# Sending a quarter of one w_down tile's rows over five of the sixteen DMA engines in a decode layer

## The chip, the core and the metric

The kernel runs on one core of a Trainium2 chip. The metric is device time in microseconds (us) of one execution, and lower is better. PE is the matrix engine, DVE the vector engine, ACT the scalar engine, POOL is GpSimd, and SP is the engine whose queue issues nearly all transfers. The core's transfers are carried by 16 DMA engines, which each take the packets handed to them in order.

## What is computed

One decode step for one token, with an attention branch and a gated feed-forward branch in parallel. All data are float32.

```python
xn = layernorm(x)                                  # x: 1 x 1 x 1024
q = (xn @ wq)                                      # 32 heads of 128
k, v = last 4096 rows of the caches                # 4 key/value heads, each used by 8 query heads
a = softmax(q k^T * 128**-0.5) v @ wo              # wo: 4096 x 1024
h = gelu(xn @ w_gate) * (xn @ w_up)                # 1024 -> 3584
out = x + a + h @ w_down                           # w_down: 3584 x 1024
```

Every weight and every cache row is used once, so about 94 MB have to come from HBM, and each loaded byte is used in one product with a vector.

## The kernel before

**Loads.** All weights and caches pass through one ring of five slots in SBUF (`ring`, 128 partitions x 40960 floats). The table `PLAN` gives for each load its place in the ring and the load whose place it takes: when the work on that older load has been written out, `used` calls `load`, which issues the transfer on SP's queue. SP waits there until the engines have read the old contents. In order these are wq in two halves, keys and values in two halves interleaved with w_gate, then w_up, wo (`oa`, `ob`, then `o1`) and at the end w_down (`d0`, `d1`, `d2`). A load of 128 partitions keeps all 16 DMA engines busy.

**w_down.** Its 3584 rows are 28 tiles of 128 rows, one row of 1024 floats (4 KB) in each partition. `d0` holds tiles 0 to 15, `d1` 16 to 23 in two pieces, `d2` 24 to 27. `PIECES` cuts `d2` into tiles 24 and 25 together (8 KB in a partition), tile 26, and tile 27, which comes in three column pieces of 2 KB, 1 KB and 1 KB in a partition.

**Products with a vector.** A tile times its scalar per partition goes one of two ways. On DVE, `add_scaled` multiplies a tile by a column and adds it to the running sum `out_part` in SBUF (one instruction for a tile of 1024 columns). On PE, `accumulate_halves` or `accumulate` multiply the tile by a column of a mostly zero matrix (`hz` for h, `oz` for the heads) and sum in PSUM. `WO_KEPT` lists the even tiles of each half of wo that go to DVE beside the odd ones; `KEPT` does so for `d0`. `downs` then adds the PE sums, takes the last tiles as they land, and `store` sends the result out in four small transfers.

**Order.** The program is written out by hand, and every engine executes its own instructions in that order. `Flow` finds the reads and writes that depend on each other and puts in semaphore waits. Where one instruction needs several semaphores, further wait instructions stand ahead of it.

**Buffers.** `Pool.tile` gives tiles of the same tag the same place, one after the other. `part` holds DVE's sums over wq, w_gate and w_up; its last reader before the end is the PE work of `projected("u")`.

Of the kernel before, what the change touches and what calls it, by code (L numbers as in the profile page):

```python
# [5 lines left out]
F32 = mybir.dt.float32  # L6
# [5 lines left out]
P = 128  # L12
D = 1024
# [5 lines left out]
NR = 4  # L19
# [9 lines left out]
WIDTHS = (NB, P // 4 * SHORT)  # L29
PIECES = ((0, 16), (0, 4, 8), (0, 2, 3, 4))  # L30
KEPT = (1, 3, 5, 7, 9, 11)
WO_KEPT = ((2, 4, 6, 10, 12, 14), (2, 4, 6, 10, 12, 14))
PAIRED = 18
# [10 lines left out]
ROW = (31, 32, 95, 96)  # L44
SIZES = {"tp": 2 * NB, "acc": 2 * NB, "s": 2 * NB, "o": 2 * NB, "part": 8 * NB, "rows": 2 * NB, "pT": 2 * NB, "p": 2 * NB}

# [193 lines left out]
class Pool:  # L240
# [33 lines left out]
    (("oa", 0), 4 * SLOT, ("g", 1)), (("ob", 0), 0, ("u", 0)), (("o", 1), SLOT, ("ua", 1)),  # L274
    (("d", 0), 3 * SLOT, ("oa", 0)), (("d", 1), 0, ("ob", 0)),
    (("d", 2), SLOT, ("o", 1)),
# [3 lines left out]
def decode_layer(nc, x, k_cache, v_cache, wq, wo, w_gate, w_up, w_down, out):  # L280
# [35 lines left out]
    def load(key, at):  # L316
        kind, i = key
        src = source(*key)
        if kind in "kv":

            loaded[key] = dst = ring[:, at:at + SLOT]
            if kind == "v":
                nc.sync.dma_start(dst, src)
            else:
                for odd in range(2):
                    nc.sync.dma_start(dst[odd:P:2], src[:, odd])
            return
        rows, n = src.shape[1:]
        loaded[key] = ring[:, at:at + rows * n]
        dst = loaded[key].rearrange("p (t n) -> p t n", n=n)  # L330
        pieces = PIECES[i] if kind == "d" else (0, rows)
        for t, end in zip(pieces, pieces[1:]):
            ends = (0, n // 2, 3 * n // 4, n) if key == ("d", 2) and end == rows else (0, n)
            for cols in (slice(*cut) for cut in zip(ends, ends[1:])):
                nc.sync.dma_start(dst[:, t:end, cols], src[:, t:end, cols])

    def used(key):
# [8 lines left out]
    for j in range(NJ):  # L346
        nc.scalar.dma_start(x_rows[j:j + 1, :], x_in[j:j + 1, :])
    sizes = (CO, NR * NJ * 32, 8 * P, (TD + 1) * 32, (HQ + 1) * 32, 2 * 32)
    zeros = consts.tile([P, sum(sizes)], F32, name="zeros")
    nc.vector.memset(zeros, 0.0)  # L350
    ends = [sum(sizes[:k]) for k in range(len(sizes) + 1)]
    x_out, xz, qz, hz, oz, units = (zeros[:, a:b] for a, b in zip(ends, ends[1:]))
    xz = xz.rearrange("p (r j m) -> p r j m", j=NJ, m=32)
# [16 lines left out]


    nc.vector.memset(units[:, 0, 31:32], 1.0)
    unit = units[:, 0, :]

    same = consts.tile([P, 4, 32], F32, name="same")
    nc.vector.tensor_add(same[:, 0, :], ident[:, 0:32], ident[:, 64:96])
    nc.vector.tensor_add(same[:, 1, :], ident[:, 32:64], ident[:, 96:128])
    quad = consts.tile([P, 4], F32, name="quad")
    nc.vector.reduce_sum(quad, ident.rearrange("p (a k) -> p a k", a=4), axis=AX.X)
# [103 lines left out]
    def queries():  # L483
        q_t = work.tile([P, 2 * 4 * 4, 32], F32, name="q_t", tag="rows")
        nc.vector.transpose(q_t.rearrange("p t r -> p (t r)"), acc["q"].rearrange("p b n -> p (b n)"))
# [63 lines left out]
    def exponentials(g, s):  # L549
        p = work.tile([P, 2, NB], F32, name="p", bufs=2)  # L550
        for odd in range(2):
            nc.scalar.activation(
                p.rearrange("p b (n odd) -> p odd (b n)", odd=2)[:, odd], s[:, odd], AF.Exp,
                bias=bias[:, g, odd:odd + 1], scale=SCALE, accum_out=l[:, g, odd:odd + 1],
            )
        probs[g] = p
# [46 lines left out]
    def heads():  # L603
        o_sb = work.tile([P, 2, DH], F32, name="o_sb", tag="p", bufs=2)
        for g in range(2):
# [6 lines left out]
        yield  # L612
        own = work.tile([P, 2, 8, WIDE], F32, name="own", tag="rows")
        nc.vector.tensor_mul(
# [10 lines left out]
    g_sb = work.tile([P, 2, NB], F32, name="g_sb", tag="pT")  # L625
    h_sb = work.tile([P, 2, NB], F32, name="h_sb")

    def gelu():
        t_sb = work.tile([P, 2, NB], F32, name="t_sb", tag="rows")
        cut = [(g_sb[:, b, :n], t_sb[:, b, :n], h_sb[:, b, :n]) for b, n in enumerate(WIDTHS)]  # L630
# [15 lines left out]
    def hidden():  # L646
# [4 lines left out]
        for b, count in enumerate((LONG, SHORT)):  # L651
            rows = h_sb[:, b, :32 * count].rearrange("p (k t) -> p t k", t=count)
            nc.vector.transpose(hz[:, t:t + count, :], rows)
            t += count

    out_p = psum.tile([P, CO], F32, name="out_p", tag="o")
    half_p = psum.tile([P, NB], F32, name="half_p", tag="s")
    halves = []
    out_part = work.tile([P, D], F32, name="out_part", tag="p")
    y = work.tile([P, CO], F32, name="y")  # L660
# [49 lines left out]
    def downs():  # L710

        tiles = [loaded["d", i][:, n * D:(n + 1) * D] for i in range(3) for n in range(DOWN[i])]
        for t in KEPT:
            add_scaled(out_part, tiles[t], hz[:, t, 31:32], False)
# [41 lines left out]
    for key, _, _ in PLAN:  # L756
        kind, i = key
        if kind == "q":
            project("q", i, loaded.pop(key), range(NR), 8 * NB)
# [56 lines left out]
        elif kind[0] == "o":  # L816
            outputs(key)
            if kind == "oa":
                gated()
            elif kind == "ob":  # L820
                hidden()
        elif i == 2:
            downs()
# [29 lines left out]
```

## Time and profile before

| | before |
|---|---|
| median of 3 runs | 226.77 us (226.47 to 226.92) |
| profiled execution, its own time | 226.74 us |
| its span, first to last instruction | 225.2 us |
| PE busy | 101.3 us (45%) |
| DVE busy | 168.2 us (75%) |
| ACT busy | 16.8 us (7%) |
| POOL busy | 0.7 us |
| DMA, data queue's packets, share of 16 engines | 97.6% |
| read from HBM | 94.38 MB, 419 GB/s over the span |

The span lies inside the execution; 1.5 us of the profiled execution's time lie outside it. Busy time is the union of an engine's instructions. The DMA share is the mean over 16 engines, so that a share of 0.25 late in the span means that four of them have packets and twelve have none. A packet counts in the stretch in which it starts, which is why a short stretch can show a share a little over 1. All rows carry L237, the line of the helper through which every instruction is issued, so they are told apart by tile names: `p<-ring,zeros,p` is `add_scaled` into `out_part` (here in the place of tag `p`), `s<-ring,zeros` is `accumulate_halves`, `o<-ring,zeros` is `accumulate`. The trace shows a float32 matmul as two MATMUL and two LDWEIGHTS.

### The profile page before, as it was taken

Reading aid. Unit: us, or ns where it says so; the run is one execution under the profiler, and the core shown is the slowest. Engines: PE = TensorE matmul, PEld = TensorE weight load, DVE = VectorE, ACT = ScalarE, POOL = GpSimd, SP = SyncE. Lnnn points to the kernel's source line nnn. Section 1 sums busy time; section 2 is a strip of 40 time slices with the busy share of each in tenths; the row PEclk is TensorE's granted clock in tenths of the full one; section 3 lists DMA queues with packets and bytes.
Section 4 is the critical chain, followed back from the end, with each engine's and each line's share of the span. In section 5 each row is a group of like instructions: output and inputs, shape, how many; then the busy total and the mean of one; then the engine's idle time right before and its main releaser. Section 6 shows DMA issues by size and latency. Waiting matters only on the chain.

```text
span 225.2 us, 1136 instructions
## 1 busy us (share of the span) xinstructions
PE 101.3 (45%) x430; PEld 37.5 (17%) x430; DVE 168.2 (75%) x148; ACT 16.8 (7%) x45; POOL 0.7 (0%) x6
## 2 busy tenths in 40 slices
PE   0120000544899999799979460010016003000986
PEld 0010000111343434243424110000001000000232
DVE  7130998598905476945439969999999998998982
ACT  0120000000102040102040140000000000000000
POOL 1000000000000000000000000000000000000000
PEclk9999999999589999999999855555556655555599
DMA  9889889799997999999989989999999989988993
GB/s 373 373 384 548 373 373 559 343 402 466 442 489 326 422 460 450 390 496 407 479 357 471 469 346 458 423 450 402 448 460 396 524 384 396 524 384 375 425 409 121
DMA packets 3236, 94.44 MB, mean 419 GB/s; under 512 B 398, under 2 KB 670, under 8 KB 928
## 3 DMA queue, kind: packets, MB, share of 16 engines
q1 hardware_dynamic: 3208, 94.38, 97.6%
q8 instruction: 3, 0.05, 0.1%
q10 hardware_dynamic: 24, 0.01, 0.0%
q14 instruction: 1, 0.01, 0.0%
HBM read 94.38 MB, written 0.00 MB: 419 GB/s over the span
## 4 chain that ended last, share of the span: by engine, by line
DMA 61%; DVE 25%; PE 11%; SPq 1%; issue 0%; ACT 0%; DVEq 0%
DVE part L237 19%; DMA ring<-in_A_wq 18%; DMA ring<-in_A_k_cache 17%; DMA ring<-in_B_w_down 13%; DMA ring<-in_A_wo 13%; PE o L237 4%; PE tp L237 3%; PE s L237 3%; DVE ring L237 2%; DVE p L237 2%; PE acc L237 1%; DVE rows L237 1%; DVE pT L237 1%; SPq L237 1%; ACT pT L237 0%
## 5 line engine op out<-in xcount | busy, mean ns | idle before, releaser
L237 DVE SCALAR_TENSOR_TENSOR part<-ring,zeros,part 128x3584 f32<-128x3584 f32 (+1 forms) x16 | 65.8, 4112 | 3.7 <-DMA ring<-in_A_wq 3.4
L237 DVE SCALAR_TENSOR_TENSOR p<-ring,zeros,p 128x1024 f32<-128x1024 f32 x34 | 43.7, 1285 | 3.2 <-DMA ring<-in_B_w_down 1.3
L237 PE MATMUL s<-ring,zeros 128*32 128x512 f32 (+1 forms) x96 | 29.1, 826 | 36.6 <-DMA ring<-in_B_w_down 17.5
L237 PE MATMUL o<-ring,pT 128*128 128x512 f32 x64 | 29.1, 599 | 1.3 <-DVE pT L237 1.3
L237 PE MATMUL acc<-ring,zeros 128*32 128x512 f32 (+2 forms) x88 | 11.4, 646 | 28.6 <-DMA ring<-in_A_wq 28.6
L237 DVE STREAM_TRANSPOSE ring<-ring 128x4096 f32<-128x4096 f32 (+1 forms) x5 | 17.7, 3571 | 2.8 <-DMA ring<-in_A_k_cache 2.8
L237 PEld LDWEIGHTS s<-ring,zeros 128*32 128x32 f32 (+1 forms) x96 | 9.7, 175 | 55.5 <-DVE p L237 19.2
L237 PE MATMUL acc<-part,zeros 128*32 128x512 f32 (+1 forms) x48 | 8.4, 835 | 21.7 <-DVE part L237 21.7
L237 PE MATMUL tp<-ring,zeros 128*128 128x512 f32 (+1 forms) x40 | 15.3, 536 | 0.0
L237 PEld LDWEIGHTS o<-ring,pT 128*128 128x128 f32 x64 | 11.7, 190 | 15.9 <-issue 13.8
L237 DVE TENSOR_SCALAR part<-ring,zeros 128x3584 f32<-128x3584 f32 (+1 forms) x3 | 6.5, 2172 | 8.6 <-DMA ring<-in_A_wq 7.6
L237 DVE STREAM_TRANSPOSE pT<-p 128x1024 f32<-128x1024 f32 x4 | 5.0, 1246 | 7.0 <-PE o L237 3.9
L237 PE MATMUL tp<-p,pick 128*128 128x256 f32 x2 | 1.2, 715 | 18.3 <-DVE p L237 18.3
L237 PEld LDWEIGHTS acc<-ring,zeros 128*32 128x32 f32 x88 | 3.1, 127 | 36.2 <-issue 35.8
L237 DVE TENSOR_REDUCE m<-s 128x2 f32<-128x1024 f32 x2 | 2.4, 1224 | 8.4 <-PE s L237 8.4
L237 PEld LDWEIGHTS tp<-ring,zeros 128*128 128x128 f32 (+1 forms) x40 | 5.9, 173 | 6.3 <-issue 5.7
L237 PEld LDWEIGHTS acc<-part,zeros 128*32 128x32 f32 x48 | 1.6, 142 | 27.2 <-DVE part L237 24.0
L237 ACT ACTIVATE o_raw<-o 32x128 f32<-32x128 f32 x16 | 4.3, 269 | 20.5 <-PE o L237 20.4
L237 PE MATMUL tp<-ident,pT 2*128 2x2 f32 x4 | 0.6, 252 | 10.3 <-DMA pT<-in_A_x 10.3
L237 PE MATMUL o<-ring,zeros 128*32 128x256 f32 x64 | 4.3, 384 | 1.6 <-DMA ring<-in_B_w_down 1.6
L237 DVE TENSOR_REDUCE m<-tp 128x2 f32<-128x1024 f32 x2 | 2.4, 1224 | 3.1 <-PE tp L237 3.1
L237 ACT ACTIVATE p<-s,bias 128x512 f32<-128x512 f32 x4 | 2.8, 715 | 24.3 <-DVE bias L237 24.3
(87 smaller groups left out, 49.1 us busy)
## 6 DMA issues: line engine op xcount, KB each, us to landing
ring<-in_B_w_gate SPq DMA_DIRECT2D x2, 7168.0 KB, 28.8
ring<-in_A_k_cache SPq DMA_DIRECT2D x4, 2048.0 KB, 41.4
ring<-in_A_v_cache SPq DMA_DIRECT2D x2, 4096.0 KB, 28.0
ring<-in_A_wo SPq DMA_DIRECT2D x2, 4096.0 KB, 27.5
ring<-in_B_w_up SPq DMA_DIRECT2D x1, 7168.0 KB, 27.8
ring<-in_B_w_up SPq DMA_DIRECT2D x2, 3584.0 KB, 21.4
ring<-in_B_w_down SPq DMA_DIRECT2D x2, 2048.0 KB, 31.7
ring<-in_B_w_down SPq DMA_DIRECT2D x1, 1024.0 KB, 29.6
```

The lines of the kernel that those rows point to most:

```text
L237: return lambda *a, **k: self.flow.issue(self.engine, lambda: call(*a, **k))
```

## The change

Tile 24 (the first tile of `d2`) is loaded in another way. Of its 128 rows, those in partitions 3, 7, 11, ... (32 of them) no longer come with the tile. They come earlier, between `o1` and `d0` on SP's queue, into the buffer `part`: six transfers of 5 rows and one of 2 rows, each row 4 KB. A transfer of 5 rows is meant for DMA engines 0 to 4, one row each, and the one of 2 rows for engines 0 and 1. The other 96 rows of the tile come in two transfers, one of 64 partitions (every second) and one of 32 (1, 5, 9, ...); the 32 missing partitions are set to zero by POOL ahead of them. So the first piece of `d2` becomes tile 24 alone, and tiles 25 and 26 come together.

The moved rows get their own product: `where`, a 0/1 matrix that POOL builds at the start, brings the h values of these rows to the partitions in which they now lie (one small matmul, `hidden_moved`, and one copy by ACT into `moved_h`), and DVE adds them to `out_part` with one more `add_scaled` on 64 partitions, ahead of those for `d0`. POOL sets `part` to zero before the rows come in.

`WO_KEPT` for the second half of wo loses tiles 4, 10 and 12, which go to PE. The kernel no longer asks for a DMA scratch of 4096 bytes for GpSimd and takes the default. To make room, buffers share places: `hz` lies over `qz`, the two buffers of tag `p` become `p0` and `p1` and also hold what `rows`, `h_sb` and `out_part` held, and `own` lies in `y`.

```diff
-PIECES = ((0, 16), (0, 4, 8), (0, 2, 3, 4))
+PIECES = ((0, 16), (0, 4, 8), (0, 1, 3, 4))
-WO_KEPT = ((2, 4, 6, 10, 12, 14), (2, 4, 6, 10, 12, 14))
+WO_KEPT = ((2, 4, 6, 10, 12, 14), (2, 6, 14))
...
+OWN, EACH, STEP = 5, 7, 4
+AWAY = 1
...
-    (("d", 0), 3 * SLOT, ("oa", 0)), (("d", 1), 0, ("ob", 0)),
+    (("m", 0), None, ("ub", 1)), (("d", 0), 3 * SLOT, ("oa", 0)), (("d", 1), 0, ("ob", 0)),
...
+        if kind == "m":
+            load_moved()
+            return
...
+        if key == ("d", 2):
+            nc.gpsimd.memset(loaded[key][:, :AWAY * n], 0.0)
+            for t, end in zip(pieces, pieces[1:2]):
+                part_of = src[:, t:end].rearrange("p t n -> p (t n)")
+                for some in (slice(0, P, 2), slice(1, P, 4)):
+                    nc.sync.dma_start(loaded[key][some, t * n:end * n], part_of[some])
+            pieces = pieces[1:]
...
+    def load_moved():
+        moved.append(work.tile([P, AWAY, D], F32, name="moved", tag="part"))
+        there = moved[0].rearrange("p t n -> p (t n)")
+        nc.gpsimd.memset(there[:64], 0.0)
+        rest = w_down[P * LONG:, :].rearrange("(p r) n -> p (r n)", r=SHORT)[STEP - 1::STEP]
+        cols = slice(DOWN[1] * D, (DOWN[1] + AWAY) * D)
+        for j in range(EACH):
+            rows = rest[OWN * j:min(OWN * j + OWN, P // STEP), cols]
+            to = 32 * (j // 4) + j % 4
+            nc.sync.dma_start(there[to:to + 4 * rows.shape[0]:4], rows)
...
-    sizes = (CO, NR * NJ * 32, 8 * P, (TD + 1) * 32, (HQ + 1) * 32, 2 * 32)
+    sizes = (CO, NR * NJ * 32, 8 * P, 32, (HQ + 1) * 32, 2 * 32)
...
+    where = consts.tile([P, 2, 8, 4], F32, name="where")
+    nc.gpsimd.memset(where, 0.0)
+    taken = ident[:, STEP - 1::STEP]
+    for j in range(EACH):
+        rows = taken[:, OWN * j:min(OWN * j + OWN, P // STEP)]
+        nc.gpsimd.tensor_copy(where[:, j // 4, :rows.shape[1], j % 4], rows)
...
+    def hidden_moved():
+        h_p = small("h_p")
+        t = DOWN[0] + DOWN[1]
+        r = slice(0, 64)
+        nc.tensor.matmul(
+            h_p[r, :AWAY], where.rearrange("p h e j -> p (h e j)"), hz[:, t:t + AWAY, 31],
+            start=True, stop=True,
+        )
+        nc.scalar.activation(moved_h[r], h_p[r, :AWAY], AF.Copy)
...
+        n = 64
+        for s in range(AWAY):
+            add_scaled(out_part[:n], moved[0][:n, s], moved_h[:n, s:s + 1], False)
         for t in KEPT:
             add_scaled(out_part, tiles[t], hz[:, t, 31:32], False)
...
-        nc = bacc.Bacc(
-            "TRN2", target_bir_lowering=False, num_devices=1, dynamic_dma_scratch_size=4096
-        )
+        nc = bacc.Bacc("TRN2", target_bir_lowering=False, num_devices=1)
```

What this does to SP's queue from the last load of wo on, before:

```order
L237 DMA ring<-in_A_wo 128x16384 [waits flow_e_DVE]
L237 DMA ring<-in_B_w_down 128x16384 [waits flow_e_PE,flow_e_DVE]
L237 DMA ring<-in_B_w_down 128x4096 [waits flow_e_PE,flow_e_DVE]
L237 DMA ring<-in_B_w_down 128x4096 [waits flow_e_DVE]
L237 DMA ring<-in_B_w_down 128x2048 [waits flow_e_PE,flow_e_DVE]
L237 DMA ring<-in_B_w_down 128x1024 [waits flow_e_DVE]
L237 DMA ring<-in_B_w_down 128x512 [waits flow_e_DVE]
L237 DMA ring<-in_B_w_down 128x256 x2
```

The same stretch of SP's queue in the changed kernel:

```order
L239 DMA ring<-in_A_wo 128x16384 [waits flow_e_DVE]
L239 DMA part<-in_B_w_down 5x1024 [waits flow_e_Pool]
L239 DMA part<-in_B_w_down 5x1024 x5
L239 DMA part<-in_B_w_down 2x1024
L239 DMA ring<-in_B_w_down 128x16384 [waits flow_e_PE,flow_e_DVE]
L239 DMA ring<-in_B_w_down 128x4096 [waits flow_e_PE,flow_e_DVE]
L239 DMA ring<-in_B_w_down 128x4096 [waits flow_e_DVE]
L239 DMA ring<-in_B_w_down 64x1024 [waits flow_e_Pool]
L239 DMA ring<-in_B_w_down 32x1024
L239 DMA ring<-in_B_w_down 128x2048 [waits flow_e_DVE]
L239 DMA ring<-in_B_w_down 128x512 [waits flow_e_DVE]
L239 DMA ring<-in_B_w_down 128x256 x2
```

Seven small transfers stand ahead of `d0` and wait for POOL, and the first piece of `d2` has become two transfers of 64 and 32 rows that wait for POOL too.

On DVE, from the turning of h into columns (`STREAM_TRANSPOSE zeros`) to the sum of the halves, before:

```order
L237 STREAM_TRANSPOSE zeros<-h_sb 128x384
L237 SCALAR_TENSOR_TENSOR p<-ring,zeros,p 128x1024 [waits flow_d_294,flow_e_DVE]
L237 SCALAR_TENSOR_TENSOR p<-ring,zeros,p 128x1024 [waits flow_e_DVE] x13
L237 SCALAR_TENSOR_TENSOR p<-ring,zeros,p 128x1024 [waits flow_d_316,flow_e_DVE]
L237 SCALAR_TENSOR_TENSOR p<-ring,zeros,p 128x1024 [waits flow_e_DVE] x5
L237 TENSOR_TENSOR p<-p,s 64x512 [waits flow_e_DVE,flow_e_PE]
```

And in the changed kernel, where `p_0` is now the place of `out_part`:

```order
L239 STREAM_TRANSPOSE zeros<-p_0 128x384
L239 SCALAR_TENSOR_TENSOR p_0<-ring,zeros,p_0 128x1024 [waits flow_d_303,flow_e_DVE]
L239 SCALAR_TENSOR_TENSOR p_0<-ring,zeros,p_0 128x1024 [waits flow_e_DVE] x10
L239 SCALAR_TENSOR_TENSOR p_0<-part,moved_h,p_0 64x1024 [waits flow_d_319,flow_d_318,flow_d_320,flow_d_317,flow_d_321,flow_d_316,flow_e_Activation,flow_d_315,flow_e_DVE]
L239 SCALAR_TENSOR_TENSOR p_0<-ring,zeros,p_0 128x1024 [waits flow_d_333,flow_e_DVE]
L239 SCALAR_TENSOR_TENSOR p_0<-ring,zeros,p_0 128x1024 [waits flow_e_DVE] x5
L239 TENSOR_TENSOR p_0<-p_0,s 64x512 [waits flow_e_DVE,flow_e_PE]
```

Three tiles of wo have left DVE here, and the product of the moved rows has come in between wo and `d0`, behind nine semaphores.

On PE, from the second part of wo to the last halves, before (`s` is the place of the halves):

```order
L237 MATMUL s<-ring,zeros 32x512 [waits flow_d_294]
L237 MATMUL s<-ring,zeros 32x512 x3
L237 MATMUL s<-ring,zeros 32x512 [waits flow_d_316,flow_e_DVE]
L237 MATMUL s<-ring,zeros 32x512 x19
L237 MATMUL s<-ring,zeros 32x512 [waits flow_e_DVE,flow_d_328]
```

And in the changed kernel:

```order
L239 MATMUL tp<-zeros,where 64x1 [waits flow_e_Pool,flow_e_DVE]
L239 MATMUL s<-ring,zeros 32x512 [waits flow_d_303]
L239 MATMUL s<-ring,zeros 32x512 x9
L239 MATMUL s<-ring,zeros 32x512 [waits flow_d_333]
L239 MATMUL s<-ring,zeros 32x512 x19
L239 MATMUL s<-ring,zeros 32x512 [waits flow_d_347]
```

Six matmuls for the three tiles of wo and the small one for `moved_h` have been added ahead of `d0`; behind it the row is as it was.

## Rows read from the trace of the kernel before

**Rows 1.** The page: DMA share in 40 slices, and the data queue's packets.
```profile
DMA  9889889799997999999989989999999989988993
...
q1 hardware_dynamic: 3208, 94.38, 97.6%
```

**Rows 2.** Chain that ended last, in order of time: start us, us, what.
```profile
159.05 29.93 DMA ring<-in_A_wo
...
191.70 30.17 DMA ring<-in_B_w_down
...
221.92 0.64 PE o L237 x8
...
223.68 0.29 DVE y_last L237
```

**Rows 3.** Timeline, PE at the end: start, us, instruction, count [idle before <-what ended it].
```profile
218.16 1.50 PE L237 MATMUL o<-ring,zeros 128*32 128x256 f32 x24 [0.91 <-DMA ring<-in_B_w_down]
...
220.66 1.07 PE L237 MATMUL o<-ring,zeros 128*32 128x256 f32 x16 [0.47 <-DMA ring<-in_B_w_down]
...
221.92 0.64 PE L237 MATMUL o<-ring,zeros 128*32 128x256 f32 x8 [0.19 <-DMA ring<-in_B_w_down]
...
223.22 0.14 PEld L237 LDWEIGHTS acc<-ring,zeros 128*32 128x32 f32 x4 [0.18 <-DMA ring<-in_B_w_down]
```

**Rows 4.** Stretches, last loads: us, engines' busy time (count), PEclk, DMA share, GB/s.
```profile
220.60:220.90 0.30, 0.24 (x5) 0.16 (x8) 0.00 (x0) 0.00 (x0) 0.00 (x0) 1.00 1.04 359
...
221.10:221.30 0.20, 0.20 (x8) 0.13 (x4) 0.00 (x0) 0.00 (x0) 0.00 (x0) 1.00 0.27 92
...
221.75:222.00 0.25, 0.08 (x4) 0.08 (x8) 0.00 (x0) 0.00 (x0) 0.00 (x0) 1.00 0.22 82
...
222.30:222.60 0.30, 0.30 (x12) 0.04 (x7) 0.00 (x0) 0.00 (x0) 0.00 (x0) 1.00 0.20 68
222.60:222.90 0.30, 0.30 (x9) 0.12 (x9) 0.27 (x1) 0.00 (x0) 0.00 (x0) 1.00 0.05 17
```

**Rows 5.** Instruction fetches, packets, MB, share: whole span, then 70:80, 85:95, 212:222.
```profile
q8 instruction: 3, 0.05, 0.1%
q14 instruction: 1, 0.01, 0.0%
...
q8 instruction: 1, 0.02, 0.6%
...
q14 instruction: 1, 0.01, 0.2%
...
q8 instruction: 1, 0.02, 0.7%
```

**Rows 6.** Timeline, DVE from the last part of wo on.
```profile
189.07 18.45 DVE L237 SCALAR_TENSOR_TENSOR p<-ring,zeros,p 128x1024 f32<-128x1024 f32 x14 [0.82 <-DMA ring<-in_A_wo]
208.43 7.89 DVE L237 SCALAR_TENSOR_TENSOR p<-ring,zeros,p 128x1024 f32<-128x1024 f32 x6 [0.90 <-DMA ring<-in_B_w_down]
```

**Rows 7.** Timeline, PE's reading of part, SP's issue of w_down, one issue alone.
```profile
167.87 3.21 PE L237 MATMUL acc<-part,zeros 128*32 128x512 f32 x16 [15.42 <-DVE part L237]
...
176.43 17.87 SPq L237 DMA_DIRECT2D ring<-in_B_w_down  x8
...
223.47 0.32 SPq L237 DMA_DIRECT2D out_y<-y  x1
```

**Rows 8.** Groups on POOL: operation, shape, count | busy us, mean ns | idle before.
```profile
L237 POOL MEMSET ident<- 128x128 f32 x1 | 0.2, 205 | 0.3 <-POOLq L839 0.3
...
L839 POOL MEMSET const-float32-0.0<- 128x1 f32 x1 | 0.1, 99 | 0.2 <-issue 0.2
```

**Rows 9.** Stretches between fetches: first two counts are PE matmuls and weight loads.
```profile
75.72:122.67 46.95, 44.00 (x130) 17.86 (x129) 29.68 (x27) 7.68 (x24) 0.00 (x0) 1.00 1.00 430
...
217.00:225.20 8.20, 5.06 (x80) 1.85 (x72) 3.30 (x7) 0.00 (x0) 0.00 (x0) 1.00 0.53 207
```

More of the change, by code (lines that the diff above doesn't have):

```diff
@@ L44 @@
 ROW = (31, 32, 95, 96)
-SIZES = {"tp": 2 * NB, "acc": 2 * NB, "s": 2 * NB, "o": 2 * NB, "part": 8 * NB, "rows": 2 * NB, "pT": 2 * NB, "p": 2 * NB}
+OWN, EACH, STEP = 5, 7, 4
+AWAY = 1
+SIZES = {"tp": 2 * NB, "acc": 2 * NB, "s": 2 * NB, "o": 2 * NB, "part": 8 * NB, "pT": 2 * NB, "p0": 2 * NB, "p1": 2 * NB}
 ISSUED = ("s", 0)
@@ L335, in load @@
                 nc.sync.dma_start(dst[:, t:end, cols], src[:, t:end, cols])
+    moved = []
+    moved_h = consts.tile([P, AWAY], F32, name="moved_h")
+    def load_moved():
[8 more added lines that the diff above has]
+            nc.sync.dma_start(there[to:to + 4 * rows.shape[0]:4], rows)
     def used(key):
@@ L351, in decode_layer @@
     ends = [sum(sizes[:k]) for k in range(len(sizes) + 1)]
-    x_out, xz, qz, hz, oz, units = (zeros[:, a:b] for a, b in zip(ends, ends[1:]))
+    x_out, xz, qz, _, oz, units = (zeros[:, a:b] for a, b in zip(ends, ends[1:]))
+    hz = zeros[:, ends[4] - (TD + 1) * 32:ends[4]]
     xz = xz.rearrange("p (r j m) -> p r j m", j=NJ, m=32)
@@ L369, in decode_layer @@
     nc.vector.memset(avg, 1.0 / D)
+    nc.gpsimd.memset(moved_h, 0.0)
     nc.vector.memset(units[:, 0, 31:32], 1.0)
@@ L483, in queries @@
     def queries():
-        q_t = work.tile([P, 2 * 4 * 4, 32], F32, name="q_t", tag="rows")
+        q_t = work.tile([P, 2 * 4 * 4, 32], F32, name="q_t", tag="p0")
         nc.vector.transpose(q_t.rearrange("p t r -> p (t r)"), acc["q"].rearrange("p b n -> p (b n)"))
@@ L549, in exponentials @@
     def exponentials(g, s):
-        p = work.tile([P, 2, NB], F32, name="p", bufs=2)
+        p = work.tile([P, 2, NB], F32, name="p", tag=f"p{(g + 1) % 2}")
         for odd in range(2):
@@ L603, in heads @@
     def heads():
-        o_sb = work.tile([P, 2, DH], F32, name="o_sb", tag="p", bufs=2)
+        o_sb = work.tile([P, 2, DH], F32, name="o_sb")
         for g in range(2):
@@ L612, in heads @@
         yield
-        own = work.tile([P, 2, 8, WIDE], F32, name="own", tag="rows")
+        own = work.tile([P, 2, 8, WIDE], F32, name="own", tag="y")
         nc.vector.tensor_mul(
@@ L625, in decode_layer @@
     g_sb = work.tile([P, 2, NB], F32, name="g_sb", tag="pT")
-    h_sb = work.tile([P, 2, NB], F32, name="h_sb")
+    h_sb = work.tile([P, 2, NB], F32, name="h_sb", tag="p0")
     def gelu():
-        t_sb = work.tile([P, 2, NB], F32, name="t_sb", tag="rows")
+        t_sb = work.tile([P, 2, NB], F32, name="t_sb", tag="p1")
         cut = [(g_sb[:, b, :n], t_sb[:, b, :n], h_sb[:, b, :n]) for b, n in enumerate(WIDTHS)]
@@ L658, in decode_layer @@
     halves = []
-    out_part = work.tile([P, D], F32, name="out_part", tag="p")
+    out_part = work.tile([P, D], F32, name="out_part", tag="p1")
     y = work.tile([P, CO], F32, name="y")
@@ L757, in decode_layer @@
         kind, i = key
+        if kind == "m":
+            continue
         if kind == "q":
```

1 line of the change is left out of this document (added).

## The prediction, made before the changed kernel was run

> **What bounds the kernel now.** I read the page first. The DMA line stands at 7 to 9 tenths in every slice but the last, and the data queue's packets fill 97.6% of 16 engines' time [rows 1]: the kernel is a stream of weights, and compute only has to keep up. Next the chain of work that ended last. From 159 us on it is two long transfers, wo until 189 us (159.05 + 29.93 = 188.98) and w_down until 221.9 us (191.70 + 30.17), and then small steps on PE and DVE up to 224 us [rows 2]. So I looked at the end alone. PE there starts four times, and each time it was idle before and a transfer of w_down ended the idle time, the last at 223.2 us [rows 3]. What sets the end is the landing of the last pieces.
>
> A load has landed when the last engine that carries it has finished, so the next view is the DMA share in short stretches. Until 220.9 us all 16 engines have packets (share 1.04). From 221.1 us on the share is 0.27, then 0.22, then 0.20, and 0.05 after 222.6 us [rows 4]. A share of 0.25 is four engines of 16 and one of 0.19 is three. So **twelve engines are done at about 221.1 us, and four still work**, three of them until 222.6 us or later. The end waits for four late engines that run some 0.8 to 1.5 us behind.
>
> What made them late? Besides data there are four larger packets in the span, of kind instruction: three on queue 8 with 16 KB each and one on queue 14 with 8 KB [rows 5]. In a window of 10 us one takes 0.6% or 0.7% of 16 engines, which is 0.006 x 160 us = 0.96 us to 1.12 us, and the small one 0.2%, 0.3 us [rows 5]. Four such packets and four late engines fit together: each delays the one engine that carries it, and in a full stream the delay stays until the end. Between two fetches PE executes 130 + 129 = 259 instructions [rows 9], so those on queue 8 look like PE's code.
>
> The Trainium skill tells this otherwise. Its page "Runtime: NRT & Kernel Launch", section "Instruction fetch mechanics", has it that crossing a 16 KiB block of code costs one tail bump that is mostly hidden. The row above gives it about 1 us of one DMA engine, and here such an engine ends last; by the page there would be no late engine to relieve, and the sum below would be zero.
>
> **The price of a row.** The piece with one tile takes PE's wait from 220.66 to 221.92 us, 1.26 us [rows 3]. It has 128 rows of 4 KB, and 524 KB in 1.26 us is 416 GB/s, the rate of the full stream, so all 16 engines carry it with 8 rows each: 1.26 / 8 = **0.158 us for a row of 4 KB**. The piece before, with 8 KB in a partition, took 220.66 - 218.16 = 2.50 us [rows 3], 0.156 us for 4 KB, so cutting it in two costs nothing that can be seen.
>
> **The change part by part.**
>
> *The rows that leave.* 32 rows of tile 24 leave the tile's transfer. Spread evenly that is 2 rows less on each engine, 2 x 0.158 = 0.315 us less ahead of everything that lands last. The late engines gain this in full if they are none of those that carry the moved rows. The 96 that stay are 4 + 2 rows on each engine, so the split into 64 and 32 leaves no engine uneven.
>
> *The rows that come.* Of seven transfers, six with 5 rows and one with 2, engines 0 and 1 get 7 rows and engines 2 to 4 get 6. Net they carry 5 or 4 rows more, 5 x 0.158 = 0.79 us or 0.63 us. If they are among the twelve that finish at about 221.1 us, they now finish at 221.7 to 221.9 us, while the late ones come from 222.6 us and more to 222.3 us and more. That cover holds about 0.4 us. The trace of before has no transfer of five rows. Each lies between its bytes, 0.158 us, and a whole issue of SP, 0.32 us [rows 7], were the engines to wait for every one. By the upper bound engines 0 and 1 would end at 221.1 + 7 x 0.32 - 0.315 = 223.0 us, and the kernel would take 226.6 to 226.7 us. I take the bytes, since the transfers are queued many us ahead of their turn, behind wo.
>
> The skill speaks against this form. "DMA: Bandwidth & Descriptors", section "Rules for kernel authors", wants an outermost dimension that is a multiple of 16, since a transfer with five rows is confined to five engines. Were all 16 to end together, that would cost the 0.79 us of engines 0 and 1 and give 227.5 us; by the share above they do not end together.
>
> *Which engines are late.* No view names an engine. Drawn at random, four late ones would all miss the five with a chance of 11 x 10 x 9 x 8 / (16 x 15 x 14 x 13) = 0.18. But single packets in the trace, which no view prints, follow one another so closely on an engine that they can be chained by their times. In these chains the two engines that carry the small loads of x were among the first five to begin the first load, and they took none of the fetches; those that took one began it late, as far as they can be told apart. I take the first five to be engines 0 to 4 and give 0.85 to their being free.
>
> *SP's queue.* The moved transfers wait for POOL, which waits until PE has read `part`, at 167.87 + 3.21 = 171.1 us [rows 7]. POOL's memset of 1024 columns: 99 ns for one column and 205 for 128 [rows 8] make 0.83 ns for a column, so 0.95 us; should it take three times that, 2.9 us. Seven issues at 0.32 us are 2.2 us [rows 7]. So they are through at 174.3 us, at worst at 176.2 us; `d0` was issued at 176.43 us [rows 7] and is needed only when wo has landed, at 189 us [rows 2]. Cost 0, with 12 us of cover. The memset ahead of tile 24 waits for PE's reading of the first tile of `o1`, soon after 189 us; `d0` alone keeps the engines busy until 208 us. Cost 0.
>
> *`d0` and `d1`.* Engines 0 to 4 are up to 7 x 0.158 = 1.1 us late in these, less than the late four, so their landing does not move.
>
> *DVE.* Three products leave and one comes. From 189.07 us 14 took 18.45 us, 1.32 each, and then DVE waited 0.90 us for `d0` [rows 6]. Now 11 + 1 take 15.8 us, with eight more wait instructions some 0.5 us: done at 205.4 us, and `d0` is there at 208.4 us. The gain of 2 us becomes waiting. Had the three tiles of wo stayed, DVE would have been late for `d0` by about 0.9 us.
>
> *PE, ACT, POOL at the start, shared places, GpSimd's scratch.* PE's six matmuls more, the one for `moved_h` and its copy stand between 188 and 208 us, where PE has nothing else. All users of a shared place are on DVE in the same order or tens of us apart. POOL's copies at the start and the shorter memset of `zeros` lie under the first load. GpSimd issues no transfers. All cost 0.
>
> **The sum.** -0.315 us on each of the last three landings; PE and DVE only waited for them, so the end moves with them. The profiled execution took 226.74 us, which gives 226.43; the median of the runs is 0.03 us higher: **226.45 us**, 0.14% less. This kernel's measurement tells apart about 0.2%, 0.45 us.
>
> **The rivals.**
>
> *One of engines 0 to 4 is a late one.* Then that engine, already last, gets 4 or 5 rows more: +0.63 or +0.79 us, 227.4 to 227.5 us. It decides as soon as one of the five ends more than 0.4 us after the twelve. For it speaks the random draw of above, against it the chains. Sixteen engines that end level would give the same time, which the falling share excludes. 0.10.
>
> *The tail is not carried over from the fetches*, but made anew by the small pieces at the end, as the skill's hidden fetch would have it. Then two rows fewer before them change nothing that lasts: 226.7 us. Against it: the share falls to whole numbers of engines, four and three, as many as there were fetches. 0.13.
>
> *A fifth fetch.* Seven matmuls more are 28 instructions in the trace (two passes, each with its weights). Behind the third fetch stood 80 + 72 = 152 instructions [rows 9]; 180 is under 259, so PE should need none. If another queue does, and on a late engine, it costs 0.96 to 1.12 us against the gain: 227.4 to 227.6 us. 0.05.
>
> **How the numbers follow.** The forecast keeps 0.72. It lies 0.13 us above the bound of faster (226.32 us), while three runs of before lay 0.45 us apart, so some three tenths of it, 0.22, count as faster, and the rest, 0.50, as no change. With the second rival that is 0.63 for within 0.2%; the first and the third make 0.15 for slower. For the range I take the forecast with the scatter of the runs on both sides, which also takes in the second rival, and the upper bound of the small transfers: 226.05 to 227.0 us. The two slower rivals are left out.
>
> **What would show it.** The idle time that a transfer ends before PE's last weights should end at about 222.9 us instead of 223.2. In the short stretches at the end the share should fall in more steps: seven engines leave first, then five some 0.6 to 0.8 us after their old time, then the late four. Four instruction packets should stand there as before, and DVE should wait about 3 us for `d0`. If the last landing comes at 223.8 us or later, a late one was among engines 0 to 4. If the landing of `d0` moves, or DMA shows a gap at 174 to 190 us, the cover on SP's queue was wrong.

## The result, and the profile after

The changed kernel takes 227.22 us (226.99 to 227.72) where the kernel before, beside it, takes 226.60 us (226.47 to 226.92). The ratio is 1.0027, with a 95% interval of 1.0018 to 1.0036: slower by 0.41 to 0.82 us. The forecast was 226.45 us and no change that can be measured.

The profiled execution of after took 227.22 us, against 226.74 us before. Its span is 0.34 us longer (225.52 against 225.18 us), and 0.14 us more lies outside the span (1.70 against 1.56 us). So there are two losses to find, and one of them is in no view of the trace.

The page of after, as [rows 1] and the first two lines of [rows 5]: DMA share in 40 slices, and the queues' packets.

```profile
span 225.5 us, 1187 instructions
...
DMA  9889889899998999997998999999999899998992
...
q1 hardware_dynamic: 3256, 94.38, 97.5%
q8 instruction: 3, 0.05, 0.1%
...
q14 instruction: 1, 0.01, 0.0%
```

The stream is as before, and so are the four fetches of code. Now the last stretches, which answer to [rows 4] (after; columns as there: PE, PEld, DVE, ACT, POOL busy with counts, PEclk, DMA share, GB/s).

```profile
221.10:221.30 0.20, 0.00 (x0) 0.00 (x0) 0.00 (x0) 0.00 (x0) 0.00 (x0) 1.00 0.45 164
...
221.75:222.00 0.25, 0.16 (x4) 0.16 (x8) 0.00 (x0) 0.00 (x0) 0.00 (x0) 1.00 0.27 94
...
222.30:222.60 0.30, 0.30 (x12) 0.21 (x8) 0.00 (x0) 0.00 (x0) 0.00 (x0) 1.00 0.07 24
222.60:222.90 0.30, 0.30 (x16) 0.21 (x10) 0.00 (x0) 0.00 (x0) 0.00 (x0) 1.00 0.01 3
```

At 221.1 us seven engines still work (0.45 x 16) where four did. At 222.3 us it is one (0.07 x 16), where three did. So most of the engines that were last are now done earlier, and the tail of the transfers is thinner, as intended. Yet the end is later. The chain that ended last shows where it runs (after; start, us, what), and the sums of y behind it stand in the timeline.

```profile
158.85 29.95 DMA ring<-in_A_wo
...
193.02 28.77 DMA ring<-in_B_w_down
...
221.84 1.11 PE o L239 x16
...
222.98 0.43 DVE y L239
...
224.02 0.29 DVE y_last L239
```

Timeline of after, PE, PEld, DVE and SP's queue at the end (start, us, instruction, count [idle before <-what ended it]), as [rows 3].

```profile
218.41 1.50 PE L239 MATMUL o<-ring,zeros 128*32 128x256 f32 x24 [0.82 <-DMA ring<-in_B_w_down]
...
221.84 1.07 PE L239 MATMUL o<-ring,zeros 128*32 128x256 f32 x16 [0.96 <-DMA ring<-in_B_w_down]
222.51 0.34 PEld L239 LDWEIGHTS tp<-ring,zeros 128*32 128x32 f32 x8
...
222.84 0.44 PEld L239 LDWEIGHTS acc<-ring,zeros 128*32 128x32 f32 x8
222.95 0.61 PE L239 MATMUL acc<-ring,zeros 128*32 128x128 f32 x8
222.98 0.42 DVE L239 TENSOR_TENSOR y<-o,zeros 128x256 f32<-128x256 f32 x1 [3.23 <-PE o L239]
223.51 0.29 DVE L239 TENSOR_TENSOR y<-y,tp 128x128 f32<-128x128 f32 x1
223.71 0.59 DVE L239 TENSOR_TENSOR y_last<-y,acc 64x128 f32<-64x128 f32 x2
...
224.34 0.25 SPq L239 DMA_DIRECT2D out_y<-y_last  x1
```

The same steps of DVE and of SP's queue in the timeline of before.

```profile
222.63 0.42 DVE L237 TENSOR_TENSOR y<-o,zeros 128x256 f32<-128x256 f32 x1 [3.13 <-PE o L237]
...
223.16 0.29 DVE L237 TENSOR_TENSOR y<-y,tp 128x128 f32<-128x128 f32 x1
...
223.36 0.61 DVE L237 TENSOR_TENSOR y_last<-y,acc 64x128 f32<-64x128 f32 x2
...
224.00 0.26 SPq L237 DMA_DIRECT2D out_y<-y_last  x1
```

Behind 221.84 us the view lists no wait of PE for a transfer: the weight loads for `tp` and `acc` have no idle time in front, where before the last ones waited until 223.22 us [rows 3]. PE is done with `acc` at 222.95 + 0.61 = 223.56 us, 0.46 us before DVE's last sum starts at 224.02 us. What is late is DVE's first sum of y, by 222.98 - 222.63 = 0.35 us, and the last store with it, by 0.34 us. That sum needs all matmuls of the piece that landed at 221.8 us. Before, this piece was one tile, with 8 matmuls and 0.64 us; now it is two, with 16 and 1.07 us. The tile taken out of the middle has pushed the other two into one piece, `PIECES` (0, 1, 3, 4), and two tiles' matmuls now stand behind the last large landing.

### The profile page after: what moved, and what is told of

Read it like the earlier page. It is cut to its first block, busy times and chain, and to the rows that moved or that the text cites. A ratio compares the mean times of both kernels' runs of the same rounds, so it can differ in the third digit from the quotient of the medians.

```text
span 225.5 us, 1187 instructions
## 1 busy us (share of the span) xinstructions
PE 106.2 (47%) x444; PEld 38.7 (17%) x444; DVE 165.0 (73%) x146; ACT 16.9 (8%) x46; POOL 4.2 (2%) x17
## 4 chain that ended last, share of the span: by engine, by line
DMA 61%; DVE 24%; PE 12%; SPq 1%; issue 1%; POOL 0%; ACT 0%; DVEq 0%
DVE part L239 19%; DMA ring<-in_A_wq 18%; DMA ring<-in_A_k_cache 17%; DMA ring<-in_A_wo 13%; DMA ring<-in_B_w_down 13%; PE s L239 4%; PE o L239 4%; PE tp L239 3%; DVE ring L239 2%; DVE p L239 1%; DVE pT L239 1%; SPq L239 1%; PE acc L239 1%; DVE o_sb L239 1%; POOL ring L239 0%
## 5 line engine op out<-in xcount | busy, mean ns | idle before, releaser
L239 DVE SCALAR_TENSOR_TENSOR p<-ring,zeros,p 128x1024 f32<-128x1024 f32 x31 | 39.8, 1285 | 6.0 <-DMA ring<-in_B_w_down 4.2
L239 PE MATMUL s<-ring,zeros 128*32 128x512 f32 (+1 forms) x108 | 32.1, 852 | 16.6 <-DMA ring<-in_B_w_down 14.6
L239 PE MATMUL acc<-part,zeros 128*32 128x512 f32 (+1 forms) x48 | 10.1, 989 | 21.5 <-DVE part L239 21.5
L239 PE MATMUL tp<-o_sb,pick 128*128 128x256 f32 x2 | 1.2, 714 | 18.4 <-DVE o_sb L239 18.4
```

The lines of the kernel that those rows point to most:

```text
L239: return lambda *a, **k: self.flow.issue(self.engine, lambda: call(*a, **k))
```

## The experiments

A kernel's time outside the span is the mean of time minus span over all its executions. Spans are on record to 0.1 us, so single values scatter by 0.05 us and the means are what counts. For before the mean was 1.57 to 1.58 us in the three comparisons that follow, with 226.69 to 226.76 us as its median; for the changed kernel, in its own nine executions, 1.71 us.

**One tile in a piece.** The first theory is that the 0.34 us come from two tiles behind the last large landing.

```diff
 (after)
-PIECES = ((0, 16), (0, 4, 8), (0, 1, 3, 4))
+PIECES = ((0, 16), (0, 4, 8), (0, 1, 2, 3, 4))
```

> The changed kernel with tiles 25 and 26 in two pieces of their own. Theory A (two tiles in the last large piece): PE has one tile, 0.64 us, behind the last large landing, not two, 1.07 us; the last start of PE moves to the last landing again, the span is 0.3 to 0.4 us shorter than the changed kernel's 225.5 us, and the time about 226.85 us against 227.2. Theory B (only the late engine among 0 to 4 counts): the last landing stays where it is, and so do the span and the time.

226.82 us, ratio 1.0009 [0.9996, 1.0023]. Eight executions took 226.58 to 226.94 us, with spans of 225.05 us in the mean, and four 227.45 to 227.90 us. Before's executions lie between 226.54 and 227.41 us without such a gap; the shorter two thirds of them have spans of 225.10 us in the mean, so the eight are no shorter than these by more than 0.05 us. The profiled execution is the longest of all (timeline of e1, then a stretch):

```profile
218.68 2.56 PE L239 MATMUL o<-ring,zeros 128*32 128x256 f32 x24 [2.01 <-DMA ring<-in_B_w_down]
...
223.66 0.42 DVE L239 TENSOR_TENSOR y<-o,zeros 128x256 f32<-128x256 f32 x1 [3.65 <-PE o L239]
```

```profile
219.00:220.00 1.00, 1.00 (x16) 0.50 (x12) 1.00 (x1) 0.00 (x0) 0.00 (x0) 0.50 1.00 388
```

PE had idled 2.01 us, and the granted clock then stood at 0.50 (1.2 GHz), so 24 matmuls took 2.56 us instead of 1.50 and the first sum of y came at 223.66 us. That belongs to no theory here; it is taken up at the end. The profile decides nothing on the piece. The eight shorter executions and the median, 0.40 us under after's and close to the 226.85 us expected, speak for the theory, and the next two runs test it without this disturbance in the sum.

**No moved rows.** All that belongs to the moved rows is taken out of after (transfers, memsets, `where`, its matmul, copy and product), and `d2` comes whole; `PIECES` stays (0, 1, 3, 4).

```diff
 (after)
-    (("m", 0), None, ("ub", 1)), (("d", 0), 3 * SLOT, ("oa", 0)), (("d", 1), 0, ("ob", 0)),
+    (("d", 0), 3 * SLOT, ("oa", 0)), (("d", 1), 0, ("ob", 0)),
...
-        for s in range(AWAY):
-            add_scaled(out_part[:n], moved[0][:n, s], moved_h[:n, s:s + 1], False)
...
-                hidden_moved()
```

> The changed kernel with tile 24 loaded whole in one transfer over all engines, and no moved rows, no memsets and no product for them; pieces, shared places, scratch and the tiles of wo stay. Theory A: the two tiles stay behind the last large landing, which comes as late as before, so the span stays at about 225.5 to 225.6 us. Theory B: the late landings of the moved rows are gone, and span and time are those of the kernel before, 225.2 and 226.6 us. The landing of d0 should be back at 208.3 us in both.

227.06 us, 1.0012 [1.0003, 1.0020]. Timeline of e2, DVE and PE:

```profile
208.31 3.92 DVE L239 SCALAR_TENSOR_TENSOR p<-ring,zeros,p 128x1024 f32<-128x1024 f32 x3 [4.86 <-DMA ring<-in_B_w_down]
...
221.84 1.07 PE L239 MATMUL o<-ring,zeros 128*32 128x256 f32 x16 [1.31 <-DMA ring<-in_B_w_down]
...
222.98 0.42 DVE L239 TENSOR_TENSOR y<-o,zeros 128x256 f32<-128x256 f32 x1 [3.58 <-PE o L239]
```

Without a single moved row the sum of y starts at 222.98 us, exactly as in after. Their piece lands at the same time too, since PE starts on it at 221.84 us in both. So the moved rows neither cause the longer span nor shorten it here; why they don't shorten it, the probe of the engines below shows. The time outside the span is back at 1.57 us.

**Before with that one number.** The opposite: only the pieces of `d2` are changed in the kernel before.

```diff
 (before)
-PIECES = ((0, 16), (0, 4, 8), (0, 2, 3, 4))
+PIECES = ((0, 16), (0, 4, 8), (0, 1, 3, 4))
```

> The kernel before with its last tiles cut as in the changed kernel: tile 24 alone, then 25 and 26 together, and nothing else. Theory A: 0.35 to 0.43 us slower than before, about 227.0 us, ratio about 1.0017, with 16 matmuls on PE behind the last large landing and DVE's first sum with y at 223.0 us. Theory B: no difference, since the bytes and the last landings are the same.

227.07 us, 1.0011 [1.0002, 1.0020]. The profiled span is 225.5 us. Timeline of e3:

```profile
218.06 2.79 PE L237 MATMUL o<-ring,zeros 128*32 128x256 f32 x24 [2.15 <-DMA ring<-in_B_w_down]
...
222.97 0.42 DVE L237 TENSOR_TENSOR y<-o,zeros 128x256 f32<-128x256 f32 x1 [3.58 <-PE o L237]
```

The sum of y is at 222.97 us, and over all executions the span is 225.52 us where before has 225.22: +0.30 us from this one number. **The first loss is settled**: two tiles behind the last large landing. (PE ran at 0.50 here too at 218 us, but its matmuls behind 221.8 us ran at full clock, so the sum of y has the time of e2.)

**The second loss: outside the span.** What e2 keeps of the change (the shared places, the default scratch, PE's six matmuls for wo) costs nothing outside the span, where e2 has 1.57 us. The scratch was also tried alone, set back to 4096 bytes:

```diff
 (after)
-        nc = bacc.Bacc("TRN2", target_bir_lowering=False, num_devices=1)
+        nc = bacc.Bacc(
+            "TRN2", target_bir_lowering=False, num_devices=1, dynamic_dma_scratch_size=4096
+        )
```

> The changed kernel with GpSimd's DMA scratch at 4096 bytes again. The time outside the span was 1.56 us before and 1.70 us in the changed kernel. Theory C (the scratch makes these 0.14 us): time 227.05 us at the same span, 1.56 us outside. Theory D (the eight transfers and semaphores more make them): 1.70 us outside and 227.2 us, as the changed kernel.

227.25 us, 1.0017 [1.0009, 1.0026], with 1.71 us outside: the scratch does nothing. This is the changed kernel's own time once more, beside other executions of before. Next POOL's late work, its two memsets behind 169 us, put on DVE:

```diff
 (after)
-            nc.gpsimd.memset(loaded[key][:, :AWAY * n], 0.0)
+            nc.vector.memset(loaded[key][:, :AWAY * n], 0.0)
...
-        nc.gpsimd.memset(there[:64], 0.0)
+        nc.vector.memset(there[:64], 0.0)
```

> The changed kernel with the two late memsets (of part at 170 us and of tile 24's place at 191 us) on DVE, so that POOL ends with its work at about 3.5 us. The time outside the span was 1.70 to 1.71 us in the kernels in which POOL has the new work, and 1.56 to 1.59 us in the others, one of which has 15 transfers more. Theory E (late work of POOL costs it): 1.57 us outside, span 225.5 us, 227.1 us. Theory F (the number of POOL's instructions costs it, 25 against 12): 1.70 us, 227.2 us. DVE waits some 3 us for PE before the first memset, which the idle time ahead of d0 should take.

227.33 us, 1.0030 [1.0018, 1.0042], 1.70 us outside. Then POOL's early work, the building of `where`:

```diff
 (after)
-    nc.gpsimd.memset(moved_h, 0.0)
+    nc.vector.memset(moved_h, 0.0)
...
-    nc.gpsimd.memset(where, 0.0)
+    nc.vector.memset(where, 0.0)
...
-        nc.gpsimd.tensor_copy(where[:, j // 4, :rows.shape[1], j % 4], rows)
+        nc.vector.tensor_copy(where[:, j // 4, :rows.shape[1], j % 4], rows)
```

> The changed kernel with the early new work of POOL (two memsets and seven copies for where) on DVE, which is idle there, and the two late memsets left on POOL. Theory E: 1.70 us outside the span, 227.2 us. Theory F: 1.60 us or less outside, 227.1 us. The span should be 225.5 us in both.

227.14 us, 1.0020 [1.0011, 1.0030], 1.72 us outside. POOL is not it, and e9 below, with all of its new work on DVE, has 1.69 us. What is left of after's additions is the matmul for `moved_h`, the transfers, DVE's one product, and ACT's one copy. ACT's copy to DVE:

```diff
 (after)
-        nc.scalar.activation(moved_h[r], h_p[r, :AWAY], AF.Copy)
+        nc.vector.tensor_copy(moved_h[r], h_p[r, :AWAY])
```

> The changed kernel with the copy into moved_h on DVE instead of ACT. In the kernels so far the time outside the span was 1.56 to 1.59 us where ACT has as many instructions as before, and 1.69 to 1.71 us where it has this one more. Theory G (the one more on ACT): 1.57 us outside at a span of 225.5 us, 227.1 us. Theory H (the three tiles and the small matmul more on PE): 1.70 us, 227.2 us.

227.10 us, 1.0015 [1.0005, 1.0024], and **1.59 us outside**. In reverse, one ACT copy of 128 values, whose result nobody reads, added to the kernel before:

```diff
 (before)
+    spare = work.tile([P, 1], F32, name="spare")
...
                 hidden()
+                nc.scalar.activation(spare, hz[:, 24, 31:32], AF.Copy)
```

> The kernel before with one more ACT instruction, a copy of one column of hz into a spare place behind the turning of h. Theory G: 1.70 us outside the span of 225.2 us, 226.9 us. Theory H: 1.56 us, as before, 226.75 us.

226.80 us, 1.0003 [0.9993, 1.0012], and **1.70 us outside**. The page of e11 and the timeline of its ACT at this place:

```profile
span 225.1 us, 1137 instructions
```

```profile
187.89 0.20 ACT L237 ACTIVATE spare<-zeros 128x1 f32<-128x1 f32 x1 [53.42 <-DVE zeros L237]
```

In the total the ratio shows nothing: e11's spans average 225.10 us, 0.09 us below before's in the same comparison, since none of its ten executions is among the long ones. The medians lie 0.11 us apart (226.80 and 226.69). In the part outside the difference is plain: executions of e11 lie at 1.66 to 1.73 us and those of before at 1.52 to 1.63, without overlap. Last, PE's extra matmuls in the kernel before:

```diff
 (before)
-WO_KEPT = ((2, 4, 6, 10, 12, 14), (2, 4, 6, 10, 12, 14))
+WO_KEPT = ((2, 4, 6, 10, 12, 14), (2, 14))
```

> The kernel before with four tiles of the second half of wo (4, 6, 10, 12) on PE instead of DVE, 16 MATMUL more in the trace, and nothing else. Theory G: 1.56 us outside the span. Theory H: 1.70 us. The span should stay at 225.2 us in both, since DVE waits for d0 anyway; the time is then 226.75 or 226.9 us.

226.76 us, 0.9999 [0.9990, 1.0009], 1.57 us outside, span 225.19 us against 225.19. PE's extra work costs nothing, as forecast. **The second loss is the one ACT copy**: 0.12 us outside the span, both when it is added (1.57 to 1.70 us, e11) and when it is removed (1.71 to 1.59 us, e10). What of it costs outside the span stays open: that ACT has one instruction more, or that it has one 53 us after its others.

**Which engines are late.** Before's w_down stream, with 15 transfers of 1 to 15 rows of 64 bytes behind `o1`. A transfer of k rows lands when its latest engine has reached it.

```diff
 (before)
...
+        for k in range(1, 16):
+            probes.append(work.tile([P, 16], F32, name="pr" + "abcdefghijklmno"[k - 1]))
+            nc.sync.dma_start(probes[-1][:k], w_down[P * k:P * k + k, :16])
...
+        for k, probe in enumerate(probes):
+            nc.vector.tensor_copy(seen[:k + 1], probe[:k + 1])
```

> The kernel before with 15 small transfers more behind the last load of wo on SP's queue, of 1, 2, 3, up to 15 rows of 64 bytes (tiles pra to pro), each of which uses as many DMA engines from engine 0 on as it has rows. A transfer lands when the latest of its engines has passed the load of wo, so the landing jumps at the row count that first takes in a later engine. Theory A (one of the four late engines is among 2 to 4): the transfers of 1 and 2 rows land at about 187.3 us, and one of those of 3, 4 or 5 rows lands 0.7 to 1.0 us later; the others of the late ones show further on. Rival (the five are free, and the moved rows were slow for another reason): no jump up to 5 rows. Time outside the span: with 15 transfers more it should be 1.56 + 15/8 x 0.14 = 1.8 us if each transfer costs there, 1.56 us if not.

227.48 us in one execution (226.86 us for before); 1.58 us outside (1.56 us for before), so 15 more transfers and semaphores are not the second loss. The single landings are in the trace's semaphore records, which no view prints, so they rest on this text. Each transfer has one landing more than the one before it, the first of a new engine; engines are numbered here by the row that they carry, from 0. For the first five these come at 187.80 (engine 0), 187.65 (1), 187.15 (2), **188.36 (3)** and 187.31 us (4); for the 13th and the 14th (engines 12 and 13) at 188.83 and 189.22 us. So one of the five, engine 3, is a late one, 0.56 us behind the next of them, though 0.86 us ahead of the latest. Each 64-byte row cost its engine about 0.18 us. The changed kernel's own records agree: its first transfer of five rows has four landings at 187.22 to 187.37 us and the fifth at 188.44, and the one of two rows, on engines 0 and 1, lands at 188.43 and 188.50 us while the late engine's rows come until 189.38.

The views show the same from the other side, in the landing of `d0`. With rows on engines 0 to 4, DVE starts on `d0` at 208.44 to 208.88 us (after, e1, e4, e6, e7 and e10; mean 208.65). Without them it starts at 208.14 to 208.48 us (before, e2, e3, e11 and e12; mean 208.33). So one of engines 0 to 4, with its rows, has become the last one for `d0`, by 0.32 us. If that is engine 3, rows on engines 0 to 2 alone leave `d0` where it was:

```diff
 (after)
-PIECES = ((0, 16), (0, 4, 8), (0, 1, 3, 4))
+PIECES = ((0, 16), (0, 4, 8), (0, 1, 2, 3, 4))
...
-OWN, EACH, STEP = 5, 7, 4
+OWN, EACH, STEP = 3, 6, 8
...
-                for some in (slice(0, P, 2), slice(1, P, 4)):
+                for some in (slice(0, P, 2), slice(1, P, 4), slice(3, P, 8)):
```

> The changed kernel with 16 rows (every eighth partition) moved to engines 0 to 2 alone, in five transfers of 3 rows and one of 1, and tiles 25 and 26 in pieces of their own. Theory (engine 3 was the late one that the moved rows hit, and a moved row costs 0.195 us, not 0.158): d0 lands at 208.2 us again instead of 208.56; engine 0 carries 6 x 0.195 - 0.158 = 1.0 us more and ends at 222.7 us; the late ones carry one row less and the last landing is at 223.0 us against 223.17 before; span 225.05 us, and with 1.70 us outside 226.75 us, as the kernel before. Rival (another engine of 0 to 2 is late, or the cost lies elsewhere): d0 lands at 208.5 us or later and the span stays at 225.3 us or more.

227.34 us (four executions of 226.81 to 227.03 us and five of 227.34 to 227.58), 1.0023 [1.0014, 1.0033], 1.72 us outside; the 226.75 us forecast for the theory are missed. Timeline of e8, DVE, PE and PEld:

```profile
208.15 3.93 DVE L239 SCALAR_TENSOR_TENSOR p<-ring,zeros,p 128x1024 f32<-128x1024 f32 x3 [3.54 <-DMA ring<-in_B_w_down]
...
218.35 2.79 PE L239 MATMUL o<-ring,zeros 128*32 128x256 f32 x24 [2.56 <-DMA ring<-in_B_w_down]
...
223.42 0.14 PEld L239 LDWEIGHTS acc<-ring,zeros 128*32 128x32 f32 x4 [0.17 <-DMA ring<-in_B_w_down]
```

`d0` is back, at 208.15 us. But the last weights come at 223.42 us, 0.20 us later than in before [rows 3], though 16 rows have left tile 24, one for each engine. `d2` is cut into more transfers here (tile 24 in three, and tiles 25 and 26 apart). The semaphore records have the last landing at 223.38 us; e1, which cuts 25 and 26 in the same way, has it at 223.38 us too, after at 223.10 us and before at 223.17 us. That the cuts cost the difference is likely, but they weren't tried alone. And PE fell to 0.50 behind a pause of 2.56 us. The same kernel with all new POOL work on DVE:

```diff
 (after, with the lines of the last diff)
-            nc.gpsimd.memset(loaded[key][:, :AWAY * n], 0.0)
+            nc.vector.memset(loaded[key][:, :AWAY * n], 0.0)
...
-    nc.gpsimd.memset(where, 0.0)
+    nc.vector.memset(where, 0.0)
...
```

> The kernel with 16 rows on engines 0 to 2, with all of the new work of POOL on DVE. If both theories hold (rows on engines that are not late, and POOL's work paid for outside the span), it is the sum: span 225.05 us, 1.57 us outside, 226.6 us, 0.15 us under the kernel before, a ratio of 0.9993. If POOL's work is not the cause of the time outside: as the kernel with 16 rows and POOL, 226.75 us.

227.03 us, 1.0012 [1.0003, 1.0021], 1.69 us outside, `d0` at 208.36 us. Both forecasts, 226.6 and 226.75 us, are missed. The semaphore records have the last landing at 223.35 us, again not earlier. No variant is faster than before. One that wasn't tried is e1 without ACT's copy: by e1's eight shorter executions and before's time outside an estimate is 225.05 + 1.58 = 226.63 us, where the shorter two thirds of before's take 226.68 us in the mean. These measurements can't tell that from no change.

## The prediction, point by point

**What bounds the kernel: right in kind, wrong in place.** The late engines are real, and the fetches made them. That is in the trace's records of single packets and landings, which no view prints. In before the 16 landings of a load lie within 0.48 us of each other until 61 us (60.86 to 61.34). A fetch starts at 75.72 us, and at the next load one landing, 79.81 us, is 1.5 us behind the others (77.93 to 78.29); behind the fetch of 8 KB at 88.6 us a second one is late (98.43 us, 0.7 us), behind the one at 122.7 us a third, and only behind the one at 217.0 us the fourth. None of them catches up. Each is later by more than its packet took, 1.03 us for the first and 0.31 us for the second, and why stays open. Three of the four did end earlier in after: the share at 222.3 to 222.6 us fell from three engines to one, and the records of landings, for the last piece, have the four late ones at 222.31, 222.96, 223.11 and 223.17 us before and at 222.52, 222.66, 222.69 and 223.10 us in after. By order of lateness the first is engine 3, which went from 222.31 to 223.10 us, and the other three gained 0.44 to 0.48 us, even more than the 0.315 us forecast. That also decides against the second rival, a tail that is made anew at the end. It speaks against the rule quoted in the prediction from the Trainium skill, page "Runtime: NRT & Kernel Launch", section "Instruction fetch mechanics", that crossing a block of code is mostly hidden: what a fetch delays here stays until the end.

**The step that failed is the sum**: "-0.315 us on each of the last three landings; PE and DVE only waited for them, so the end moves with them". Neither half of it held. The last large piece has PE's start behind it at 221.84 us instead of 221.92, and the last landing of all went from 223.17 to 223.10 us: 0.07 to 0.08 us, because engine 3 was late (below). And the end hung on more than those landings. [Rows 2] show the chain of before as far as the landing at 221.92 us and PE's 8 matmuls; the next steps are these.

```profile
222.56 0.42 PE tp L237 x8
222.98 0.67 PE acc L237 x8
```

The last weights for `acc` did wait for the landing of 223.2 us [rows 3]. But DVE's sums of y were as late by themselves. In after, where PE has long finished `acc`, the four start 0.53, 0.20 and 0.31 us apart (222.98, 223.51, 223.71, 224.02 us); in before 0.53, 0.20 and 0.32 us apart (222.63, 223.16, 223.36, 223.68 us). So two paths that differ by about 0.01 us ended there, and shortening the one through the last landing could have gained no more than that. The other path, through the first sum of y, was lengthened by an edit costed at nothing. "Cutting it in two costs nothing" was said of the transfer, and the question was what PE has left when the last large piece lands: [rows 3] have both prices, 1.07 us for 16 matmuls and 0.64 us for 8. Their difference of 0.43 us, less the landing 0.08 us earlier, is the 0.35 us of the sum of y.

**A row that comes: mis-sized.** It was put at 0.158 us, with 0.32 us as upper bound. In after the landings of the transfers of five follow each other by 0.18 to 0.20 us in the semaphore records (187.22, 187.42, 187.62, 187.82, 188.00, 188.18 us for the earliest engine; 188.44 to 189.38 us in five steps for engine 3). So engine 3 got 6 x 0.19 = 1.14 us more ahead of `d0`, and net 1.14 - 0.315 = 0.82 us at the end, where 0.79 us is what it shows.

**"I take the first five to be free": wrong**, engine 3 was among the late ones. It was the least late of them, so the first rival's mechanism came true without its price: the last landing moved by -0.07 us (223.17 to 223.10 us), neither by -0.315 nor by +0.63 us. That it hardly moved at all is chance: engine 3 lost 0.79 us and had been 0.86 us ahead of the latest. At the last large piece engine 3 lands at 221.80 us in after and the next latest at 221.41, so this one engine took back some 0.4 us that the others had gained. At the end eight engines are done by 221.39 us, four by 222.21, then the last four, where the prediction wanted seven, five and four. "The landing of `d0` does not move" fell with it, by 0.2 to 0.3 us, which DVE and PE pay for out of slack; the cover on SP's queue, which the prediction would have blamed for that sign, held. The rule of the Trainium skill that was weighed there, page "DMA: Bandwidth & Descriptors", section "Rules for kernel authors", agrees with the trace as to place, since a transfer of five rows lands in five parts and no more. The 0.79 us that the prediction worked out from rows for 16 engines that end together did not come, since they don't end together.

**"All cost 0": wrong for ACT's copy**, and nothing else in that list was found to cost time. The copy adds 0.12 us outside the span, where I had not looked: the prediction took the 1.5 us outside as a constant. PE's matmuls (e12), the scratch (e4) and POOL (e6, e7) cost nothing to be seen.

**SP's queue and DVE: right as to the end, with one price mis-sized.** Timeline of after, POOL, SP's queue and DVE:

```profile
169.67 0.94 POOL L239 MEMSET part<- 64x1024 f32 x1 [166.24 <-PE acc L239]
...
170.64 5.09 SPq L239 DMA_DIRECT2D part<-in_B_w_down  x7
...
176.24 18.79 SPq L239 DMA_DIRECT2D ring<-in_B_w_down  x9
...
203.43 1.28 DVE L239 SCALAR_TENSOR_TENSOR p<-part,moved_h,p 64x1024 f32<-64x1024 f32 x1
...
208.66 7.89 DVE L239 SCALAR_TENSOR_TENSOR p<-ring,zeros,p 128x1024 f32<-128x1024 f32 x6 [3.95 <-DMA ring<-in_B_w_down]
```

The memset took 0.94 us (forecast 0.95). The seven transfers took SP 5.09 us to issue, 0.73 us each, instead of 2.2; they were through at 175.7 us, still ahead of `d0`'s old time of issue [rows 7]. DVE was done at 204.7 us (forecast 205.4) and waited 3.95 us for `d0` (forecast 3).

**Together**: +0.34 us in the span and +0.14 us outside make +0.48 us in the profiled executions. The measured ratio is +0.41 to +0.82 us, and e4, the same work, +0.20 to +0.59 us; before's median was 226.60 us in the first comparison and 226.76 us in that of e4. What after's longer executions (up to 227.72 us) have beyond that stays open, as they have no traces. In e1, e9 and e10 the profiled execution is the longest of its kernel, and in each PE's granted clock stood at 0.50 from 219 to 220 us; that the same happened in after's is possible and not shown.

## What to carry to other kernels

When transfers set the end, list every landing of the last microseconds with the work that still follows it, and shorten the longest sum; cut the pieces so that the last large one leaves the fewest instructions, and watch the last landing, which came 0.2 us later in the kernels with more cuts (e1, e8, e9). A time has a part outside the span too, and it isn't a constant: compare time minus span before and after. Before rows are put on chosen engines, measure with small transfers which engines are late and what a row in a transfer of its own costs.

## What was not expected of the hardware

- One ACT copy of 128 values far behind ACT's other work adds 0.12 us outside the span (1.57 to 1.70 us, e11; back to 1.59 us, e10).
- In a transfer with one row for each engine a row costs its engine about 0.18 us at 64 bytes (e5) and 0.18 to 0.20 us at 4 KB (after), against 0.158 us for 4 KB where the transfer has eight rows for each engine (before).
- A fetch of code leaves the engine that carries it late until the end, by more than the packet took: 1.5 us for 1.03 us (16 KB), 0.7 us for 0.31 us (8 KB), in before.
- PE's granted clock at the end differed between the traces. In e1, e3, e8, e9 and e10 PE had been idle for 1.95 to 2.56 us ahead of 218 us; the granted clock then stood at 0.50 (1.2 GHz) from 219 to 220 us, and the next 24 matmuls took 2.40 to 2.79 us. In the other nine traces PE had been idle for 0.74 to 1.59 us there, and the 24 matmuls took 1.50 us at 1.00 (2.4 GHz). Whether the pause is what makes the difference was not tested. In e1 the first sum of y waited for PE until 223.66 us behind such a stretch.
